# A gated pair of state-space convolutions: decay powers, the negation of v, kept spectra and the gate regrouped, with a new order of work

## The chip, the cores and the metric

The kernel runs on one core of a Trainium2 chip. Such a core has a matrix engine (TensorE, PE in the profile; its weight loads are listed as PEld), a vector engine (VectorE, DVE), an engine for activation functions (ScalarE, ACT), a general one (GpSimd, POOL) and one that issues DMAs here (SyncE, SP). Each runs its own queue in order, and waits on semaphores for the others. The metric is device time of one launch in microseconds (us); less is better.

## The reference

Two state-space convolutions A and B over the same input of 2048 steps by 512 channels, mixed by a gate. Each makes its kernel K from 128 complex modes for a channel, and convolves through an FFT of twice the length:

```python
def ref(u, log_A_real, A_imag, C_real, C_imag, log_dt, D_skip):
    dt = exp(log_dt)
    A = -exp(log_A_real) + 1j * A_imag
    C = (C_real + 1j * C_imag) * dt[:, None]
    P = exp((A * dt[:, None])[:, :, None] * arange(L)[None, None, :])
    K = 2.0 * einsum("dn,dnl->dl", C, P).real
    y = irfft(rfft(u_t, 2 * L) * rfft(K, 2 * L))[..., :L]
    return y_t + u * D_skip

g = sigmoid((x * gate_w).sum(-1, keepdims=True))
return g * ref(x, A_...) + (1 - g) * ref(x, B_...)
```

All data are float32.

## The kernel before

The time axis of 2048 is split in 32 by 64, and the channels of both convolutions (2 x 512) in 64 **units** of 16. Eight units are a **chunk** (parameters of 128 channels of A and B together), two units a pair, and four units a **block**, of which there are 16.

*Parameters.* For chunk 0 alone, and then for the chunks 1 and 2, 3 and 4, 5 and 6, 7, `prep_ops` derives phases and amplitudes; for the later chunks most of it is done on GpSimd (lines 375 to 412). The phases go to DRAM and back in another layout (`bounce`, then `turns`, on the SP queue). `dec` holds two values per mode and channel: the decay rate and the amplitude.

*Bases.* `make_bases` (line 488) makes for each chunk a table `bas` of 28 columns per channel: the powers exp(-s x rate) for s = 0 to 7, 0, 8, ... 56, 0, 64, ... 448 and 0, 512, ... 1536. The zeros are set once; the 24 other columns are one Exp each on ScalarE, of 128 channels, written with a step of 28. `amplitudes` (lines 491, 493, GpSimd) puts in column 24 to 27 the amplitude.

*Units.* For each unit, `phase` (504, TensorE) makes phases in PSUM; ScalarE turns them into sines and cosines (510, 513, 516); `grid0` and `grid1` (520, GpSimd) multiply base columns to decays, 128x1024 and 128x512, into two tiles f0 and f1 of two buffers each; VectorE multiplies decays and sines (543 to 563). `modes` (571, TensorE) sums over the 128 modes, with four column tiles of 32 at a time, into a PSUM tile `pk` of 128x256. `keep` (578, ScalarE) copies it to `ks`, `skip` (581, VectorE) adds the skip weights to its first column. For a pair, `first_k` (593, TensorE) does the first stage of the transform and `keep_x` (600, ScalarE) stores it in `xall`. `inputs` loads and transforms the input of a block in the same way (`load_u` on SP, `first_u`, `keep_u`).

*Blocks.* For a block, `s2` (630, TensorE) does the second stage of the transform in 8 groups; `products` (641, VectorE) multiplies kernel and input spectra; `add_products` (669, on POOL's queue) adds their halves with accumulating DMAs; `inverse` (679, TensorE) transforms back and `keep_z` (685, ScalarE) stores. The spectra of the input, `v`, serve two blocks. They are made ahead for the blocks b + 1 and b + 2 when b is odd, and for blocks 0 and 1 at the start, 8 rounds in all: `keep_v` (650, ScalarE) copies from PSUM, `turn_v` and `both_v` move halves between partitions with DMAs of SP, and `negate_v` (661, VectorE) writes the negative of 64 partitions by 512 columns, four times in a round.

*Ends.* `gate` (760, TensorE, early in the kernel) multiplies the transposed input with the gate's weights: four matmuls for each quarter j, one after another into one PSUM bank, 128 equal output rows; then Sigmoid (765) and a product into the transform's last table (770). `final` (699) and, for the last 128 channels, `last_final` (733) do the last stage; SP writes the result.

*Order.* All this is listed as some 2460 small operations. `ORDER` is a permutation of them, written out in full; they are emitted in that order, and each engine is held to it by extra dependences. `SLOTS` names the PSUM bank, of eight, of each PSUM tile in turn.

Of the kernel before, what the change touches and what calls it, by code (L numbers as in the profile page):

```python
# [29 lines left out]
SHIFTS = list(range(8)) + [8 * b for b in range(8)] + [64 * b for b in range(8)] + [512 * b for b in range(4)]  # L30
# [4 lines left out]
    11, 2, 0, 6, 1, 3, 4, 5, 74, 15, 19, 20, 21, 23, 22, 25, 24, 29, 40, 26, 27, 45, 12, 28, 18,  # L35
    31, 30, 41, 32, 42, 33, 50, 34, 43, 35, 44, 13, 36, 37, 46, 38, 39, 55, 71, 47, 16, 48, 49,
    51, 52, 53, 70, 17, 69, 54, 56, 57, 58, 60, 14, 59, 62, 61, 63, 64, 65, 72, 66, 75, 73, 183,
    67, 83, 68, 78, 84, 82, 7, 79, 8, 85, 192, 9, 10, 147, 323, 80, 77, 210, 81, 76, 191, 86,
    194, 195, 193, 107, 109, 211, 196, 200, 111, 110, 108, 201, 197, 113, 202, 112, 198, 209,
    203, 199, 204, 114, 115, 212, 123, 127, 117, 215, 126, 205, 213, 124, 119, 216, 218, 217,  # L40
    121, 222, 120, 118, 219, 206, 122, 116, 156, 223, 149, 129, 230, 132, 214, 133, 232, 130,
    207, 221, 125, 324, 236, 128, 231, 151, 237, 150, 152, 238, 153, 348, 233, 131, 326, 134,
    157, 89, 234, 87, 158, 208, 235, 239, 90, 155, 325, 93, 243, 88, 161, 160, 220, 162, 148,
    92, 349, 244, 181, 91, 241, 163, 98, 240, 182, 224, 164, 351, 154, 99, 242, 350, 248, 159,
    225, 250, 97, 226, 245, 254, 94, 249, 251, 305, 246, 255, 103, 247, 227, 100, 307, 252, 261,
    102, 306, 229, 258, 135, 256, 96, 257, 228, 253, 262, 95, 165, 308, 260, 311, 166, 259, 104,
    309, 167, 312, 314, 101, 168, 310, 318, 263, 169, 313, 106, 316, 171, 327, 264, 319, 329,
    265, 315, 138, 333, 328, 105, 330, 317, 334, 584, 335, 340, 331, 170, 732, 341, 332, 172,
    136, 336, 175, 173, 337, 320, 338, 174, 352, 321, 354, 339, 139, 322, 137, 342, 358, 353,
    355, 141, 140, 343, 359, 344, 371, 360, 365, 356, 372, 366, 357, 361, 370, 176, 362, 144,  # L50
    177, 363, 373, 364, 178, 376, 374, 377, 379, 179, 383, 378, 741, 180, 380, 184, 375, 384,
    142, 742, 382, 266, 768, 185, 381, 145, 743, 367, 143, 268, 746, 267, 385, 747, 368, 146,
    734, 186, 748, 269, 386, 447, 187, 369, 749, 387, 736, 272, 271, 275, 270, 274, 278, 273,
    276, 281, 277, 280, 284, 283, 188, 282, 287, 286, 290, 285, 289, 279, 452, 189, 291, 453,
    292, 345, 288, 737, 735, 455, 739, 388, 448, 738, 294, 293, 346, 471, 347, 390, 389, 449,
    296, 295, 391, 395, 392, 190, 450, 399, 396, 403, 400, 744, 733, 454, 407, 456, 404, 1317,
    472, 408, 405, 457, 451, 401, 406, 397, 402, 393, 411, 398, 409, 458, 461, 740, 394, 415,
    459, 750, 413, 430, 460, 427, 412, 419, 465, 751, 410, 414, 416, 752, 745, 417, 470, 753,
    421, 418, 466, 767, 297, 473, 756, 420, 462, 476, 424, 474, 463, 299, 477, 423, 464, 478,
# [123 lines left out]
    2396, 2395, 2400, 2399, 2403, 2398, 2402, 2406, 2401, 2405, 2409, 2404, 2407, 2412, 2408,  # L183
    2410, 2415, 2411, 2414, 2312, 2417, 2416, 2413, 2314, 2313, 2421, 2315, 2418, 2419, 2420,
    2422, 2424, 2423, 2426, 2425, 2428, 2427, 2429, 2450, 2453, 2451, 2452, 2456, 2454, 2455,
    2459, 2457, 2458, 2460, 2461,
]


# [807 lines left out]
```

## Time and profile before

| what | value |
|---|---|
| median of 3 runs | 570.46 us |
| lowest and highest run | 565.07, 579.27 us |
| span of the profiled execution, first to last instruction | 568.5 us |
| mean granted TensorE clock | 0.921 of full |
| busy time of PE, DVE, ACT, POOL | 458.2, 412.8, 426.0, 342.6 us |
| HBM read and written | 17.18 and 5.77 MB |

The profile has one execution, of which it gives the span only; the span lies between the lowest and the highest run. Its views are: totals by engine, the chain that ended last (followed back from the last instruction, at each step to what released it), groups of instructions by line with busy time and idle time before them, the timeline, and busy time by stretches. In a group, the busy time is that in which at least one of its instructions ran, so that busy time by count is the pitch of instructions that overlap, while "mean ns" is the full length of one. A float32 matmul is recorded as two instructions.

### The profile page before, as it was taken

To read this page: it belongs to the slowest core of one execution; us is meant where nothing else is said; L and a number is where in the kernel's file an instruction comes from. 1 tells how busy PE (TensorE), PEld (TensorE's weight loads), DVE (VectorE), ACT (ScalarE), POOL (GpSimd) and SP (SyncE) were. 2 spreads that over 40 slices of the span, in tenths; PEclk is the share of its full clock that TensorE was granted. 3 is DMA by queue.
4 is the path that set the end of the run, shared out by engine and by line. 5 is a ranking of instruction groups with operands and counts; after the bars stand their busy time and mean duration, and the time that the engine had idled before them with its cause. 6 is when DMAs were issued, how large, how long until landed. Compare 5 with 4: busy or idle time off the path is not lost.

```text
span 568.5 us, 26964 instructions
## 1 busy us (share of the span) xinstructions
PE 458.2 (81%) x11888; PEld 371.7 (65%) x11888; DVE 412.8 (73%) x826; ACT 426.0 (75%) x967; POOL 342.6 (60%) x324
## 2 busy tenths in 40 slices
PE   8557986879777898868997986968997979859756
PEld 8445456657575676767775774856785757748746
DVE  7096876888967983798689855698689896788210
ACT  4788879969986998867997994949987777565311
POOL 1549986989999877346766653435727664455120
PEclk9797989989988997998999996989997997989779
DMA  3649423460423515044506323044505250163242
GB/s 102 216 130 315 188 58 50 105 131 22 91 48 89 110 38 114 33 98 83 110 7 134 81 51 76 32 96 91 95 21 115 40 96 22 31 131 64 44 74 77
DMA packets 30772, 49.84 MB, mean 88 GB/s; under 512 B 10048, under 2 KB 15680, under 8 KB 30656
## 3 DMA queue, kind: packets, MB, share of 16 engines
q1 hardware_dynamic: 25536, 31.34, 18.6%
q0 software_dynamic: 5120, 16.78, 17.8%
q8 instruction: 93, 1.52, 1.1%
q14 instruction: 23, 0.19, 0.1%
HBM read 17.18 MB, written 5.77 MB: 40 GB/s over the span
## 4 chain that ended last, share of the span: by engine, by line
PE 29%; ACT 17%; DVE 15%; issue 7%; POOL 5%; DMA 1%; ACTq 0%; DVEq 0%; POOLq 0%
PE pk L571 6%; PE psi L679 6%; DVE xall L641 5%; PE p0s L504 5%; DVE v L661 4%; ACT bas L488 4%; PE ps L630 4%; PE ps L593 3%; PE pf L699 3%; ACT xall L600 2%; PE pl L733 1%; ACT p1c L510 1%; ACT z L685 1%; ACT p0c L516 1%; ACT p0c L510 1%
## 5 line engine op out<-in xcount | busy, mean ns | idle before, releaser
L520 POOL TENSOR_TENSOR f<-bas 128x512 f32<-128x512 f32 (+1 forms) x128 | 203.4, 1670 | 119.1 <-PE pk L571 49.3
L630 PE MATMUL ps<-xall,gk 128*64 128x64 f32 (+1 forms) x1728 | 109.4, 252 | 13.3 <-ACT v L650 4.3
L630 PEld LDWEIGHTS ps<-xall,gk 128*64 128x64 f32 (+1 forms) x1728 | 102.4, 155 | 24.8 <-issue 6.6
L641 DVE TENSOR_TENSOR xall<-ps,v 128x256 f32<-128x256 f32 x256 | 91.4, 418 | 26.1 <-PE ps L630 21.1
L571 PE MATMUL pk<-f,f 128*32 128x64 f32 x4096 | 79.1, 231 | 23.7 <-DVE f L551 13.2
L571 PEld LDWEIGHTS pk<-f,f 128*32 128x32 f32 x4096 | 67.3, 117 | 35.0 <-issue 24.4
L669 POOL DMA_DIRECT2D xall<-xall x64 | 60.0, 1203 | 48.0 <-ACT z L685 22.6
L679 PE MATMUL psi<-mi,xall 128*128 128x128 f32 x512 | 74.8, 303 | 11.4 <-DMA xall<-xall 6.8
L679 PEld LDWEIGHTS psi<-mi,xall 128*128 128x128 f32 x512 | 67.8, 211 | 22.5 <-issue 10.7
L559 DVE TENSOR_TENSOR f<-f,p1c 128x512 f32<-128x512 f32 x64 | 43.7, 684 | 25.8 <-ACT p1c L516 23.8
L543 DVE TENSOR_TENSOR f<-f,p0c 128x512 f32<-128x512 f32 x64 | 43.6, 683 | 24.5 <-ACT p0c L516 22.6
L504 PE MATMUL p0s<-cph,ones 64*128 64x512 f16 x128 | 52.8, 412 | 9.2 <-ACT xall L600 3.9
L593 PE MATMUL ps<-w,ks 64*64 64x64 f32 x2048 | 41.9, 231 | 16.2 <-issue 8.1
L685 ACT COPY z<-psi 128x512 f32<-128x512 f32 x64 | 38.5, 620 | 21.5 <-PE psi L679 21.5
L504 PE MATMUL p1s<-cph,ones 64*128 64x512 f16 x128 | 53.0, 414 | 0.7 <-DVE f L559 0.7
L593 PEld LDWEIGHTS ps<-w,ks 64*64 64x64 f32 x2048 | 36.6, 144 | 25.3 <-issue 11.8
L504 PE MATMUL p0s<-cph,rot 64*128 64x512 f16 x128 | 52.4, 409 | 0.2 <-issue 0.2
L504 PE MATMUL p1s<-cph,rot 64*128 64x512 f16 x128 | 52.4, 409 | 0.0
L488 ACT ACTIVATE bas<-dec 128x128 f32<-128x128 f32 x192 | 50.6, 490 | 0.8 <-DVE dec L423 0.7
L510 ACT ACTIVATE p1c<-p1s 128x512 f32<-128x512 f32 x64 | 38.2, 597 | 16.9 <-PE p1s L504 8.1
L510 ACT ACTIVATE p0c<-p0s 128x512 f32<-128x512 f32 x64 | 38.8, 607 | 15.4 <-PE p1s L504 5.7
L563 DVE TENSOR_TENSOR f<-f,p1s 128x512 f32<-128x512 f32 x64 | 43.7, 684 | 5.7 <-ACT p1s L513 4.3
(130 smaller groups left out, 866.7 us busy)
## 6 DMA issues: line engine op xcount, KB each, us to landing
xall<-xall POOLq DMA_DIRECT2D x64, 256.0 KB, 5.3
v<-v SPq DMA_DIRECT2D x64, 128.0 KB, 3.3
uraw<-in_us SPq DMA_DIRECT2D x16, 256.0 KB, 4.2
z<-in_ut SPq DMA_DIRECT2D x16, 256.0 KB, 6.8
out_dram<-ot SPq DMA_DIRECT2D x24, 128.0 KB, 2.4
par<-in_par SPq DMA_DIRECT2D x8, 256.0 KB, 5.2
gk<-in_gk SPq DMA_DIRECT2D x4, 512.0 KB, 7.0
eg<-in_eg SPq DMA_DIRECT2D x4, 512.0 KB, 7.2
```

Of the source, the lines that this page charges most:

```text
L488: S.activation(bas[:, c % 2, :, j], decays[c][:, 0], AF.Exp, scale=-float(s))
L504: PE.matmul(ps, w[h : h + 64], cph[h : h + 64, j], start=j == 0, stop=j == 3, tile_position=(h, 0))
L510: S.activation(pc[u], ps[u], AF.Abs)
L520: G.tensor_tensor(o.rearrange("p k (a b) -> p k a b", b=8), x[:, :, hi : hi + n].unsqueeze(3).to_broadcast([128, 16, n, 8]), x[:, :, lo : ...
L559: V.tensor_tensor(f[:, 0], f[:, 1], p1c[u], OP.mult)
L571: PE.matmul(pk[32 * kd : 32 * kd + 32, i, :], f1[:, p, 4 * i + kd, :], f0[:, p, 4 * i + kd, :], start=p == 1, stop=p == 0, tile_position=( ...
L593: PE.matmul(ps[h][64 * ri : 64 * ri + 64, n, :], x[r], w1[r, ri, r], start=True, stop=True, tile_position=(64 * h, 64 * ri),)
L630: PE.matmul(ps[h : h + w, j, 0:n], gk[:, k, h : h + w], xall[:, x0:x1, 2 * k : 2 * k + 2], start=True, stop=True, tile_position=(0, h),)
L641: V.tensor_tensor(k.rearrange("p x (k t) -> p k x t", t=2), p2s[b, g][:, :, 0:64].rearrange("p k (x t) -> p k x t", t=2), vv.unsqueeze(3). ...
L669: G.dma_start(out=xk(b)[o, s], in_=t2[t, s], accum_op=OP.add)
L679: PE.matmul(ps[:, i, :], xk(b)[:, x : x + 2, :].rearrange("p x k -> p (x k)"), mi, start=True, stop=True)
L685: S.copy(z[:, :, d0 : d0 + 4], pis[b, g].rearrange("p i r -> p r i"))
```

## The change

- *Decay powers.* A new GpSimd product `multiples` makes 1 to 7 times the rate, 128 x 128 x 7, in a tile `rates` of one buffer. `make_bases` is then four Exps for a chunk with scales of -1, -8, -64 and -512: three write 7 columns per channel (896 elements a partition), the fourth 3 (384).
- *Negation.* `negate_v` moves to GpSimd, as a tensor_tensor product with a broadcast column of -1.
- *Kept spectra.* `modes` of the two units of a pair write one PSUM tile of 128x512; `keep` and `skip` run once per pair.
- *Gate.* The four matmuls of a quarter write 32 rows each, in four column tiles; ScalarE copies the result over the input it was made from, and one matmul with a matrix of 1/32 sums the four parts into 128 equal rows.
- *Order.* `inputs` is listed after every second unit of an odd block; `ORDER` (2422 operations now) and `SLOTS` (636 in place of 664) are new throughout.

```diff
-SHIFTS = list(range(8)) + [8 * b for b in range(8)] + [64 * b for b in range(8)] + [512 * b for b in range(4)]
...
+    thirty = const.tile([128, 128], F32, name="thirty")
+    seven = const.tile([128, 7], F32, name="seven")
+    minus = const.tile([128, 1], F32, name="minus")
...
+        V.memset(minus, -1.0)
+        for n in range(7):
+            V.memset(seven[:, n : n + 1], n + 1.0)
+        G.memset(thirty, 1.0 / 32)
...
+    def multiples(c):
+        rates[c] = work.tile([128, 128, 7], F32, name="rates", tag="rates", bufs=1)
+        G.tensor_tensor(
+            rates[c], decays[c][:, 0].unsqueeze(2).to_broadcast([128, 128, 7]),
+            seven.unsqueeze(1).to_broadcast([128, 128, 7]), OP.mult,
+        )
+
     def make_bases(c, n):
-        for j, s in list(enumerate(SHIFTS))[10 * n : 10 * n + 10]:
-            if s:
-                S.activation(bas[:, c % 2, :, j], decays[c][:, 0], AF.Exp, scale=-float(s))
+        j, w = 8 * n + 1, 7 if n < 3 else 3
+        S.activation(bas[:, c % 2, :, j : j + w], rates[c][:, :, 0:w], AF.Exp, scale=-float(8**n))
...
     def modes(u):
         f0, f1 = f0s[u], f1s[u]
-        pks[u] = pk = bank("pk")[:, 0:256].rearrange("p (i j) -> p i j", i=4)
+        q, h = divmod(u, 2)
+        if h == 0:
+            pks[q] = bank("pk", (128, 8, 64))
...
-                        pk[32 * kd : 32 * kd + 32, i, :], f1[:, p, 4 * i + kd, :], f0[:, p, 4 * i + kd, :],
-                        start=p == 1, stop=p == 0, tile_position=(0, 32 * kd),
+                        pks[q][32 * kd : 32 * kd + 32, 4 * h + i, :], f1[:, p, 4 * i + kd, :],
+                        f0[:, p, 4 * i + kd, :], start=p == 1, stop=p == 0, tile_position=(0, 32 * kd),
...
-    def keep(u):
-        kss[u] = work.tile([128, 4, Q], F32, name="ks", tag="ks", bufs=4)
-        S.copy(kss[u], pks[u])
-
-    def skip(u):
-        V.tensor_tensor(kss[u][:, :, 0], pks[u][:, :, 0], dl[:, 4 * u : 4 * u + 4], OP.add)
+    def keep(q):
+        kss[q] = work.tile([128, 8, Q], F32, name="ks", tag="ks", bufs=2)
+        S.copy(kss[q], pks[q])
+
+    def skip(q):
+        V.tensor_tensor(kss[q][:, :, 0], pks[q][:, :, 0], dl[:, 8 * q : 8 * q + 8], OP.add)
...
     def negate_v(i, h):
-        V.tensor_scalar(v_at(hi, i, 1, h), v_at(hi, i, 0, h), -1.0, None, op0=OP.mult)
+        x = v_at(hi, i, 0, h)
+        G.tensor_tensor(v_at(hi, i, 1, h), x, minus[hi].unsqueeze(2).to_broadcast(x.shape), OP.mult)
...
-    def gate(j):
+    def gate_parts(j):
         psg[j] = bank("psg")
         for sb in range(nsb):
             PE.matmul(
-                psg[j], gw[:, sb : sb + 1].to_broadcast([128, 128]), ut(sb, j), start=sb == 0, stop=sb == nsb - 1
+                psg[j][32 * sb : 32 * sb + 32], gw[:, sb : sb + 1].to_broadcast([128, 32]), ut(sb, j),
+                start=True, stop=True, tile_position=(0, 32 * sb),
             )
+
+    def gate_keep(j):
+        S.copy(ut(0, j), psg[j])
+
+    def gate(j):
+        psg[j] = bank("psg")
+        PE.matmul(psg[j], thirty, ut(0, j), start=True, stop=True)
...
     def chunk(c):
         op("ro", turns, c)
-        for n in range(3):
+        op("mu", multiples, c)
+        for n in range(4):
             op("ex", make_bases, c, n)
...
         if u % 2:
-            op("f1", first_k, u // 2)
+            q = u // 2
+            op("ke", keep, q)
+            op("kd", skip, q)
+            op("f1", first_k, q)
...
-        if b % 2 and n < 2 and b < nblk - 1:
-            inputs(b + 1 + n)
+        if b % 2 and n % 2 and b < nblk - 1:
+            inputs(b + 1 + n // 2)
```

28 lines of the change are left out of this document (10 added, 18 removed), and 293 rows, old and new, of tables (ORDER, SLOTS).

## The prediction

> **What bounds the kernel now.** I read the totals first, then the chain that ended last, then the groups of instructions and the order of time around the pieces the chain names. Totals and the chain by engine:
>
> ```profile
> span 568.5 us, 26964 instructions
> PE 458.2 (81%) x11888; PEld 371.7 (65%) x11888; DVE 412.8 (73%) x826; ACT 426.0 (75%) x967; POOL 342.6 (60%) x324
> PE 29%; ACT 17%; DVE 15%; issue 7%; POOL 5%; DMA 1%; ACTq 0%; DVEq 0%; POOLq 0%
> ```
>
> No engine is full. TensorE is busy 81% of the span, and the chain passes from engine to engine, so the time is set by waits between queues that are each run in a fixed order. The chain of waits by line:
>
> ```profile
> by line: issue 7.2%; PE pk L571 6.2%; PE psi L679 5.8%; DVE xall L641 4.6%; PE p0s L504 4.6%; DVE v L661 4.3%; ACT bas L488 4.1%; PE ps L630 3.8%; PE ps L593 3.4%; PE pf L699 3.3%; ACT xall L600 1.6%; PE pl L733 1.4%; ACT p1c L510 1.3%; ACT
> ```
>
> Two entries stand out, because they are no heavy arithmetic: the negation of v (DVE L661, 4.3% of 568.5 = 24.4 us) and the Exps of the decay powers (ACT L488, 4.1% = 23.3 us). The groups of instructions show how large they are as a whole, and give the durations used below (the columns are busy time, mean ns of one, then the idle time ahead of it):
>
> ```profile
> L520 POOL TENSOR_TENSOR f<-bas 128x1024 f32<-128x1024 f32 x64 | 136.2, 2129 | 10.4 <-ACT bas L488 6.5 <-PE pk L571 3.9
> L571 PE MATMUL pk<-f,f 128*32 128x64 f32 x4096 | 79.1, 231 | 23.7 <-DVE f L551 13.2 <-issue 8.2 <-DVE f L555 1.1
> L520 POOL TENSOR_TENSOR f<-bas 128x512 f32<-128x512 f32 x64 | 76.9, 1211 | 108.7 <-PE pk L571 45.3 <-issue 23.4 <-DVE f L543 16.9
> L488 ACT ACTIVATE bas<-dec 128x128 f32<-128x128 f32 x192 | 50.6, 490 | 0.8 <-DVE dec L423 0.7
> L661 DVE TENSOR_SCALAR v<-v 64x512 f32<-64x512 f32 x32 | 41.1, 1298 | 0.8
> L600 ACT COPY xall<-ps 128x512 f32<-128x512 f32 x64 | 36.2, 616 | 10.5 <-PE ps L593 10.3
> L578 ACT COPY ks<-pk 128x256 f32<-128x256 f32 x64 | 25.6, 402 | 28.2 <-PE pk L571 28.1
> L760 PE MATMUL psg<-z,small 128*128 128x512 f32 x32 | 14.8, 605 | 0.0
> L581 DVE TENSOR_TENSOR ks<-pk,dl 128x4 f32<-128x4 f32 x64 | 10.3, 161 | 35.3 <-ACT ks L578 34.9
> L383 POOL TENSOR_TENSOR tb<-tb,sg 128x256 f32<-128x256 f32 x12 | 10.0, 831 | 0.5
> L488 ACT ACT_TABLE_LOAD x6 | 7.7, 1283 | 0.1
> ```
>
> The negation's mean is 1298 ns, with 64 partitions by 512 columns. One that runs undisturbed takes a third of that. The order of time around unit 28 shows why:
>
> ```profile
> 247.52 0.42 DVE L661 TENSOR_SCALAR v<-v 64x512 f32<-64x512 f32 x1
> ...
> 250.66 4.79 DVE L661 TENSOR_SCALAR v<-v 64x512 f32<-64x512 f32 x2
> 250.66 1.36 POOL L520 TENSOR_TENSOR f<-bas 128x512 f32<-128x512 f32 x1
> 251.67 1.16 POOL L669 DMA_DIRECT2D xall<-xall  x1
> 252.26 2.55 POOL L520 TENSOR_TENSOR f<-bas 128x1024 f32<-128x1024 f32 x1
> ...
> 255.48 0.69 DVE L547 TENSOR_TENSOR f<-f,p0c 128x512 f32<-128x512 f32 x1
> 256.22 1.59 PE L593 MATMUL psu<-w,uraw 64*64 64x64 f32 x64 [4.46 <-DVE f L547]
> ```
>
> With POOL idle the negation takes 0.42 us (247.52). At 250.66 two of them start with a POOL grid and are over only after POOL's next 128x1024 grid has ended (252.26 + 2.55 = 254.81). The DVE does nothing else for 4.79 us, and TensorE then stands 4.46 us, released by the DVE instruction behind the negations. The same picture, three more times:
>
> ```profile
> 306.82 2.56 DVE L661 TENSOR_SCALAR v<-v 64x512 f32<-64x512 f32 x1
> 310.25 1.10 PE L571 MATMUL pk<-f,f 128*32 128x64 f32 x64 [3.51 <-DVE f L551]
> ...
> 376.33 4.78 DVE L661 TENSOR_SCALAR v<-v 64x512 f32<-64x512 f32 x2
> 381.89 1.99 PE L593 MATMUL psu<-w,uraw 64*64 64x64 f32 x64 [4.45 <-DVE f L547]
> ...
> 497.45 3.62 DVE L661 TENSOR_SCALAR v<-v 64x512 f32<-64x512 f32 x1
> 503.01 1.24 PE L593 MATMUL ps<-w,ks 64*64 64x64 f32 x36 [4.77 <-DVE f L555]
> ```
>
> **The change part by part.** The sums are made against the profiled execution's span of 568.5 us. The page gives no other time of that execution; the median of the three runs, 570.46 us, is 2.0 us above the span, and I add these 2 us at the end.
>
> *1, negation to POOL.* DVE loses all 32 L661 instructions, 41.1 us. The four stalls above cost TensorE 4.46 + 3.51 + 4.45 + 4.77 = 17.2 us of standing. TensorE stands 19% of the span anyway (100 less 81), so of these 17.2 us I count 81%, **14 us gained**. The ends: nothing, if TensorE is held by the next late thing; 24.4 us, the negation's whole share of the chain. I take 14 since it is read off TensorE itself. On POOL a negation is a tensor_tensor of 512 columns with a broadcast operand; the nearest row is the 128x512 grid, also with broadcast operands, 76.9 / 64 = 1.20 us (the plain 128x256 product's 831 ns is the lower bound, two of these the upper one). 32 x 1.20 = 38 us more on POOL.
>
> *2, Exps.* Before, a chunk needs 24 Exps of 128 columns: 50.6 / 192 = 0.263 us each when back to back, 6.3 us a chunk. After: three of 896 columns and one of 384. Between 0.263 us for 128 columns and 36.2 / 64 = 0.566 us for 512 (L600) lie 0.79 ns a column, so 0.87 us and 0.47 us, 3.1 us a chunk; by L600's mean of 616 ns for 512 columns alone, 1.08 and 0.46, 3.7 us. I take 3.4: 2.9 us saved in each of 8 chunks, 23 us of ACT. Of the 50.6 us, 23.3 are on the chain, 46%, so at most 10.7 us can come off the end; nothing, if ACT's next work waits for TensorE anyway. I take half, 5.4. The new order changes between Exp, Sin and Sigmoid 22 times where the old one did 21 times by my count of both lists (chunk 5's four Exps are cut in two by unit 32's sines), so one load of 1.28 us more. **4 us gained.** In front of the Exps stands a new POOL product of 896 columns: between the grid rows, 1.20 us at 512 and 136.2 / 64 = 2.13 us at 1024, that is 1.9 us, 15 us for 8. Its tile has one buffer, so the product for chunk 2 waits on POOL until chunk 1's four Exps are done. Behind it in POOL's queue stand the added products of block 0 and then unit 8's grids; the grids read these very Exps, so the wait adds nothing to them.
>
> The load's own row, and the Exps behind it:
>
> ```profile
> 329.52 1.28 ACT L488 ACT_TABLE_LOAD   x1
> 330.82 6.42 ACT L488 ACTIVATE bas<-dec 128x128 f32<-128x128 f32 x24
> ```
>
> The Exps start 0.02 us after the load has ended. The Trainium skill ("ScalarE: Activation LUTs", What ACT_TABLE_LOAD costs) sets 2.66 us for a switch, a load and a drain of 1.38 us. By that the extra switch would cost 1.4 us more than I count; these two rows show no such gap.
>
> *3, two units per kept spectrum.* 64 copies of 256 columns (25.6 us) become 32 of 512 at 0.566, 18 us: 7 us off ACT; 64 additions (10.3 us) become 32: 5 us off DVE. Neither line is among the chain's entries of over 1%. On the other side a PSUM bank is now held over two units, and the first unit's kernel spectrum waits for the second unit. Between 3 us either way I take **1 us gained**.
>
> *4, gate.* 16 products of 512 columns, 14.8 us of TensorE. On four column tiles, the four of a gate can run side by side: the modes (L571) do so, 64 columns in 79.1 / 4096 = 19 ns where 14.8 / 32 = 462 ns for 512 columns make 58 ns for 64. Then 3.7 us, 3.7 us for the four summing products, and four ACT copies, 2.3 us, ahead of which TensorE has other work in the new list. 7.4 us less, at most; TensorE idles 19% of the span and more work waits behind ACT and DVE there, so **1 us gained**, and 4 us lost if the tiles ran one behind the other.
>
> *5, POOL as a whole.* 38 + 15 = 53 us more. Its busy time in two stretches (the columns are PE, PEld, DVE, ACT, POOL):
>
> ```profile
> 40.00:200.00 160.00, 126.52 (x2906) 95.57 (x2908) 126.08 (x240) 137.12 (x311) 141.89 (x144) 0.94 0.43 110
> 200.00:480.00 280.00, 238.20 (x6786) 192.93 (x6787) 218.36 (x424) 223.05 (x512) 156.92 (x140) 0.92 0.35 72
> ```
>
> From 200 on POOL has 280 - 157 = 123 us to spare: the cover is there. From 40 to 200 it has 18 us. Up to unit 21, where that stretch ends, the new list puts 9 negations and 3 products there, 9 x 1.20 + 3 x 1.9 = 16.5 us. But it also moves the preparation of chunks 5 and 6 out: 25 POOL instructions stand ahead of unit 18's grids in the old list, 4 ahead of the grids of unit 21 in the new one; at 0.83 us these 21 are 17 us. So this stretch stays as full as it was. What is not covered is a grid that is due at once and now has a negation in front of it; a tenth of 53 us, **5 us lost**, between 0 and the 53 themselves.
>
> *6, the rest of the order.* All lists are new, also those of SP and of POOL's accumulating DMAs; the number of DMAs stays (156 issues of SP, 64 of POOL). Two places can be priced. Preparation for chunk 7 goes late: its bounce to DRAM and back now stands on SP behind three transfers of v of block 11, which wait for ACT's copies; it is due at unit 56, four units on, so it is covered. And the end:
>
> ```profile
> 526.12 1.50 PE L593 MATMUL ps<-w,ks 64*64 64x64 f32 x85
> 531.13 1.54 PE L593 MATMUL ps<-w,ks 64*64 64x64 f32 x43 [3.51 <-issue]
> 532.60 3.78 PE L679 MATMUL psi<-mi,xall 128*128 128x128 f32 x16
> 536.31 5.20 PE L630 MATMUL ps<-xall,gk 128*64 128x64 f32 x128
> 541.44 2.17 PE L679 MATMUL psi<-mi,xall 128*128 128x128 f32 x16
> 543.35 3.32 POOL L669 DMA_DIRECT2D xall<-xall  x4 [15.22 <-ACT z L685]
> 550.42 5.42 PE L679 MATMUL psi<-mi,xall 128*128 128x128 f32 x32 [6.82 <-DMA xall<-xall]
> ```
>
> Here all is serial: last spectra (L593), block 14's first two inverses (532.60), block 15's second stage (536.31), its products, POOL's accumulating DMA, block 15's inverses (550.42). The new list puts all four inverses of block 14 behind the second stage, where 6.82 us of waiting for the DMA cover them: 536.31 - 532.60, **3.7 us gained**. What else the order does I can't price; I put it at 10 us either way in the range.
>
> Sum: 568.5 - 14 - 4 - 1 - 1 + 5 - 3.7 = 549.8, and 2 for the median: 552 us.
>
> **The rivals.** *Hidden:* DVE and ACT are relieved, but TensorE's own work sets the pace. It falls from 458.2 to 450.8 us; at today's span per busy us, 568.5 / 458.2 = 1.24, the span is 559, the time 561. For it: PE has the largest share of the chain, 29%. Against: the four stalls stand on TensorE itself.
>
> *All of it:* the whole chain shares come off, 24.4 + 10.7 + 3.7 = 38.8, time 532. Against: with 7 to 8 us a unit on three engines, another wait is seldom far behind.
>
> *POOL blocks:* a negation must wait for ACT's copies of v, and in POOL's fixed order everything behind it waits too, the grids of the next units above all. POOL has paid for such a wait already, ahead of an accumulating DMA:
>
> ```profile
> 375.74 0.86 POOL L669 DMA_DIRECT2D xall<-xall  x1 [6.85 <-ACT v L650]
> ```
>
> If each of the 8 rounds of negations holds POOL so long, 8 x 6.85 = 55 us, the gains (23.7 without the 5 us lost) are eaten and the time is 570.5 - 23.7 + 55 = 602; it is over 2% slower from 35 us, 4.4 us a round. Against: the new list places a round's four negations apart, up to 12 units late, after the copies are due. The Trainium skill ("GPSIMD Engine Reference", Engine selection) speaks against this move as well: elementwise work belongs on VectorE, with GpSimd about twice as slow for two inputs. By that factor a negation would be 0.84 us and POOL's load 11 us smaller than mine. The rows agree with the direction, 1.20 against 0.42 us, yet the 0.42 us held only while POOL was idle.
>
> **How the numbers follow.** About 2% (11 us) is what a measurement of this kernel can tell from no change: faster is below 559, slower above 582. My forecast of 538 to 559 has 0.50, all of it (below 538) 0.14, hidden (559 to 582) 0.24, POOL blocks (over 582) 0.12. Faster is 0.50 + 0.14. The range 533 to 574 leaves out most of the blocked case, and the ends of two others.
>
> **What would show it.** In the profile after: no POOL-long DVE instruction of v; negations on POOL at 1.1 to 1.3 us; DVE busy about 367 us, ACT near 397, POOL near 395, PE near 451; Exps in groups of some 3.4 us a chunk; second stage of block 15 directly behind the last L593. I am wrong if POOL's waits for ACT's copies of v, or for TensorE's modes, grow by more than 25 us, or if TensorE's idle time stays at 110 us.

## The result, and the profile after

The changed kernel takes 509.47 us (median of 4 runs, 502.11 to 512.51), against 570.44 us of the kernel before in the same comparison (565.07 to 579.27). The ratio is 0.887, with a 95% interval from 0.877 to 0.896: 11% faster. Ratios, here and below, are made from the faster executions of each kernel alone, medians from all: for the changed kernel the faster two, 502.11 and 507.36 us, make the gain 65 us, and the profile below is of an execution of 511.58 us. By the medians it is 61 us, where 18 us were forecast; the time lies below the range (533 to 574), and 23 us below the rival that took the whole chain shares off. The direction was right, the size was not.

Totals of the changed kernel, and its chain that ended last, by engine:

```profile
span 509.8 us, 26782 instructions
PE 441.0 (87%) x11896; PEld 356.5 (70%) x11896; DVE 369.9 (73%) x770; ACT 402.7 (79%) x780; POOL 386.8 (76%) x365
PE 50%; DMA 10%; issue 10%; DVE 10%; POOL 9%; ACT 9%; SPq 0%; DVEq 0%; POOLq 0%; ACTq 0%
```

The busy times came out nearly as forecast: VectorE 369.9 us (forecast 367), ScalarE 402.7 (397), GpSimd 386.8 (395), TensorE 441.0 (451). So the work that each part moves was counted well. What was not forecast is how closely TensorE is kept fed: it is busy 87% of the span, not 81%, and half of the chain is now its own, not 29%. The groups of the parts that changed (busy time, mean ns of one, idle time before):

```profile
L653 POOL TENSOR_TENSOR v<-v,minus 64x512 f32<-64x512 f32 x32 | 33.1, 1042 | 8.4 <-issue 6.4
L470 POOL TENSOR_TENSOR rates<-dec,seven 128x896 f32<-128x896 f32 x8 | 14.5, 1812 | 0.0
L477 ACT ACTIVATE bas<-rates 128x896 f32<-128x896 f32 x24 | 22.2, 969 | 0.1
L477 ACT ACTIVATE bas<-rates 128x384 f32<-128x384 f32 x8 | 5.0, 620 | 0.0
L569 ACT COPY ks<-pk 128x512 f32<-128x512 f32 x32 | 19.8, 618 | 14.2 <-PE pk L562 14.2
L572 DVE TENSOR_TENSOR ks<-pk,dl 128x8 f32<-128x8 f32 x32 | 5.3, 167 | 7.0 <-ACT ks L569 6.8
L752 PE MATMUL psg<-z,small 128*32 128x512 f32 x32 | 5.1, 704 | 0.0
L762 PE MATMUL psg<-z,thirty 128*128 128x512 f32 x8 | 6.3, 882 | 0.0
L562 PE MATMUL pk<-f,f 128*32 128x64 f32 x4096 | 76.3, 226 | 14.0 <-issue 9.1 <-ACT p1s L502 2.1 <-DVE f L552 1.2
L509 POOL TENSOR_TENSOR f<-bas 128x1024 f32<-128x1024 f32 x64 | 134.5, 2112 | 28.7 <-PE pk L562 17.7 <-issue 10.4
L509 POOL TENSOR_TENSOR f<-bas 128x512 f32<-128x512 f32 x64 | 78.1, 1226 | 19.8 <-issue 8.5 <-PE pk L562 7.2 <-DVE xall L632 3.1
```

A negation on GpSimd takes 1.03 us by its pitch (33.1 / 32; forecast 1.20), a product of rates 1.81 (forecast 1.9), the Exps 27.2 us for 8 chunks (22.2 + 5.0), which is 3.4 a chunk as forecast. The gate takes 5.1 + 6.3 = 11.4 us of TensorE, 3.4 less than before and not 7.4 less. That is in part the clock: one of the four quarters and two of the four sums ran at a granted clock of 0.50 to 0.56 and took 1.85 to 2.07 us each, the others 1.06 to 1.13 us at 1.00. In a run below with the same gate (e3) the two lines take 4.3 and 4.5 us. The last two rows show how GpSimd makes room: it stands 19.8 + 28.7 = 48.5 us ahead of its grids, where it stood 108.7 + 10.4 = 119.1 us before, although it has 44 us more to do. By the same two rows it stands 94.2 us with the old work in the new order (e1) and 79.8 us with the negation alone moved in the old one (e7), so the order and the negation both have a part in this.

Where TensorE stands behind VectorE's multiplications, the longest groups before (above) and after (below), from the view of waits: total us, times, longest:

```profile
PE pk L571 <- DVE f L551: 13.2, 6, 3.6
PE psu L593 <- DVE f L547: 8.9, 2, 4.5
PE psu L593 <- DVE f L559: 6.7, 2, 6.3
PE ps L593 <- DVE f L555: 4.8, 1, 4.8
```

```profile
PE ps L621 <- DVE f L540: 1.3, 2, 0.7
PE pk L562 <- DVE f L552: 1.2, 3, 0.4
PE p1s L493 <- DVE f L548: 0.8, 1, 0.8
```

Added up over all rows of that view, by the engine and the tile named as releaser, TensorE's idle time in the kernels that the text below compares is (us; "mult." are VectorE's multiplications into f, "issue" is time in which the profile shows no wait; waits too short for a row are left out, so that busy and idle time come to a few us less than the span):

```
kernel (profiled run)                  span  PE busy  PE idle | mult. issue  ACT   DMA  DVE ks  clock
before                                568.5   458.2    104.4  |  44.6  24.1  19.2  12.2   0.9   0.921
old order, three parts (e2)           567.2   451.2    111.0  |  26.6  31.6  24.0  20.3   5.3   0.925
old order, negation on GpSimd (e7)    559.4   452.6    101.6  |  26.3  27.7  18.9  21.4   3.4   0.930
old order, four Exps (e9)             571.4   457.0    108.9  |  44.4  28.5  19.2  12.8   0.6   0.922
old order, products regrouped (e12)   578.1   462.8    109.5  |  32.4  28.3  20.6  19.0   3.9   0.914
old order, preparation spread (e13)   609.5   471.2    132.7  |  49.2  25.8  26.1  12.3  16.1   0.888
new order, old work (e1)              535.1   456.6     72.7  |  19.9  18.9   9.7  10.2   6.7   0.946
after                                 509.8   441.0     63.9  |   8.6  29.1  10.1   9.1   5.2   0.959
```

Of the 58.7 us between the two spans, 40.5 are idle time of TensorE and 17.2 are its busy time. Of the 17.2, the gate accounts for 3.4; in the rest the same matmuls run shorter (the 4096 records of the modes 76.3 us, 79.1 before), at a granted clock of 0.959 in place of 0.921. The clock was higher in nearly every kernel in which TensorE stood less; whether it follows from that was not tried. By the ratio of the clocks alone 458.2 us would become 440.0, near the 441.0 measured; but for the new order with the old work (e1) it gives 446.1, and 456.6 was measured. So the clock fits here, and is not the whole account.

The stretches of the prediction, after the change (columns as there: PE, PEld, DVE, ACT, POOL, then clock, DMA share, GB/s):

```profile
40.00:200.00 160.00, 137.23 (x3557) 102.33 (x3561) 130.71 (x249) 142.21 (x268) 148.87 (x141) 0.95 0.39 88
200.00:480.00 280.00, 251.01 (x7214) 206.89 (x7205) 206.45 (x419) 219.58 (x434) 207.40 (x188) 0.96 0.39 83
```

TensorE is busy 137 of 160 us from 40 to 200, where it was 127, and 251 of 280 us behind, where it was 238. The gain is not in one place: the last kept spectrum of unit 9 comes at 103.7 us (120.7 before), of unit 31 at 254.7 (285.0), of unit 63 at 476.1 (526.6), and the end at 509.8 (568.5). These are 17, 13, 20 and 8 us by stretch.

### The profile page after: what moved, and what is told of

It is laid out like the page before. It is cut to its first block, busy times and chain, and to the rows that moved or that the text cites. A ratio compares the mean times of both kernels' runs of the same rounds, so it can differ in the third digit from the quotient of the medians.

```text
span 509.8 us, 26782 instructions
## 1 busy us (share of the span) xinstructions
PE 441.0 (87%) x11896; PEld 356.5 (70%) x11896; DVE 369.9 (73%) x770; ACT 402.7 (79%) x780; POOL 386.8 (76%) x365
## 4 chain that ended last, share of the span: by engine, by line
PE 50%; DMA 10%; issue 10%; DVE 10%; POOL 9%; ACT 9%; SPq 0%; DVEq 0%; POOLq 0%; ACTq 0%
PE ps L621 14%; PE pk L562 9%; PE psi L671 8%; DMA xall<-xall 7%; PE p0s L493 6%; POOL f L509 4%; DVE xall L632 4%; PE ps L584 3%; POOL xall L661 3%; PE pf L691 3%; PE psu L584 2%; PE pl L725 2%; DMA uraw<-in_us 1%; ACT xall L591 1%; DVE f L552 1%
## 5 line engine op out<-in xcount | busy, mean ns | idle before, releaser
L509 POOL TENSOR_TENSOR f<-bas 128x1024 f32<-128x1024 f32 (+1 forms) x128 | 204.0, 1669 | 48.5 <-PE pk L562 25.0
L621 PE MATMUL ps<-xall,gk 128*64 128x64 f32 (+1 forms) x1728 | 114.0, 254 | 9.3 <-issue 3.1
L562 PE MATMUL pk<-f,f 128*32 128x64 f32 x4096 | 76.3, 226 | 14.0 <-issue 9.1
L562 PEld LDWEIGHTS pk<-f,f 128*32 128x32 f32 x4096 | 64.7, 113 | 28.0 <-issue 18.6
L671 PE MATMUL psi<-mi,xall 128*128 128x128 f32 x512 | 70.9, 288 | 8.7 <-DMA xall<-xall 2.9
L671 PEld LDWEIGHTS psi<-mi,xall 128*128 128x128 f32 x512 | 62.5, 196 | 18.3 <-issue 4.7
L536 DVE TENSOR_TENSOR f<-f,p0c 128x512 f32<-128x512 f32 x64 | 43.7, 683 | 26.1 <-ACT p0c L505 23.6
L532 DVE TENSOR_TENSOR f<-f,p0c 128x512 f32<-128x512 f32 x64 | 43.6, 681 | 10.5 <-POOL f L509 5.2
L584 PE MATMUL ps<-w,ks 64*64 64x64 f32 x2048 | 38.9, 223 | 12.1 <-issue 6.6
L584 PEld LDWEIGHTS ps<-w,ks 64*64 64x64 f32 x2048 | 34.3, 136 | 19.7 <-issue 9.2
L544 DVE SCALAR_TENSOR_TENSOR f<-f,p0s 128x512 f32<-128x512 f32 x64 | 43.6, 681 | 5.0 <-ACT p0s L502 3.9
## 6 DMA issues: line engine op xcount, KB each, us to landing
xall<-xall POOLq DMA_DIRECT2D x64, 256.0 KB, 5.8
z<-in_ut SPq DMA_DIRECT2D x16, 256.0 KB, 5.5
uraw<-in_us SPq DMA_DIRECT2D x16, 256.0 KB, 3.7
par<-in_par SPq DMA_DIRECT2D x8, 256.0 KB, 5.5
```

The costliest lines, as they stand in the source:

```text
L509: G.tensor_tensor(o.rearrange("p k (a b) -> p k a b", b=8), x[:, :, hi : hi + n].unsqueeze(3).to_broadcast([128, 16, n, 8]), x[:, :, lo : ...
L532: V.tensor_tensor(f0[:, 0, :, 0:32], f0[:, 1, :, 0:32], half(u, p0c[u], True), OP.mult)
L536: V.tensor_tensor(f0[:, 0, :, 32:64], f0[:, 1, :, 32:64], half(u, p0c[u], False), OP.mult)
L562: PE.matmul(pks[q][32 * kd : 32 * kd + 32, 4 * h + i, :], f1[:, p, 4 * i + kd, :], f0[:, p, 4 * i + kd, :], start=p == 1, stop=p == 0, til ...
L584: PE.matmul(ps[h][64 * ri : 64 * ri + 64, n, :], x[r], w1[r, ri, r], start=True, stop=True, tile_position=(64 * h, 64 * ri),)
L621: PE.matmul(ps[h : h + w, j, 0:n], gk[:, k, h : h + w], xall[:, x0:x1, 2 * k : 2 * k + 2], start=True, stop=True, tile_position=(0, h),)
```

## The experiments

*All old work in the new order (e1), and three of the four parts in the old order (e2).* Nearly the two halves of the change. e1 is the changed kernel with the parts' work put back; the pair's kernel spectra still share one PSUM tile, since the new list is written for that:

```diff
-            rates[c], decays[c][:, 0].unsqueeze(2).to_broadcast([128, 128, 7]),
...
-        S.activation(bas[:, c % 2, :, j : j + w], rates[c][:, :, 0:w], AF.Exp, scale=-float(8**n))
+        for k in range(w):
+            S.activation(bas[:, c % 2, :, j + k], decays[c][:, 0], AF.Exp, scale=-float((k + 1) * 8**n))
...
-        S.copy(kss[q], pks[q])
+        for h in range(2):
+            S.copy(kss[q][:, 4 * h : 4 * h + 4], pks[q][:, 4 * h : 4 * h + 4])
...
-        G.tensor_tensor(v_at(hi, i, 1, h), x, minus[hi].unsqueeze(2).to_broadcast(x.shape), OP.mult)
+        V.tensor_scalar(v_at(hi, i, 1, h), v_at(hi, i, 0, h), -1.0, None, op0=OP.mult)
...
+                psg[j], gw[:, sb : sb + 1].to_broadcast([128, 128]), ut(sb, j), start=sb == 0, stop=sb == nsb - 1
```

e2 is the kernel before, with its list of operations, and the changed Exps with their product, negation and gate; kernel spectra are still kept unit by unit, so that the third part is missing.

> The new order with the old work: 24 Exps of 128 columns for a chunk, the negation on VectorE as a tensor_scalar, two copies and two additions for a pair, the old gate. Theory A (the order carries what the forecast missed, some 40 us; the four parts give some 18): about 528 us, 0.925 of before. Theory B (the parts carry nearly all, the order little): 560 us or more, 0.98 or more. Theory C (the order fits only the new work, both are needed): not below 550 us here and not below 540 us with the parts alone.

> The old order with the new work of three parts: four Exps and a POOL product for a chunk, the negation on POOL, the gate on four column tiles, each at the place where the old order had the old work (kept spectra stay one unit at a time, since a bank held over two units can't be fitted to the old list of banks). Theory A: 545 to 555 us, 0.96 of before. Theory B: 510 to 525 us. Theory C: 540 to 565 us.

Measured: e1 535.39 us, ratio 0.939 (0.935 to 0.943); e2 570.07 us, ratio 1.000 (0.996 to 1.003). So 35 us come with the order (with its banks and its shared PSUM tile), nothing with three parts alone, and 61 with everything: the parts are worth 26 us by the medians, 30 by the ratios, but only in the new order. Of the theories the first came nearest for e1 (528), and none has e2's 570. In e2 the stalls behind the negation are gone as forecast (idle time behind VectorE's multiplications 44.6 to 26.6 us), and the time comes back under other names: issue +7.5, ScalarE +4.8, DMA +8.1, kept spectra +4.4.

*One part back in the changed kernel (e3, e4, e5, e6).* e3 puts the negation back on VectorE, e4 the 24 Exps of a chunk, e5 the two copies and additions of a pair, each with the lines of the diff above. e6 puts the gate's old matmuls back:

```diff
-        psg[j] = bank("psg")
-        for sb in range(nsb):
-            PE.matmul(
-                psg[j][32 * sb : 32 * sb + 32], gw[:, sb : sb + 1].to_broadcast([128, 32]), ut(sb, j),
-                start=True, stop=True, tile_position=(0, 32 * sb),
-            )
...
-        S.copy(ut(0, j), psg[j])
...
-        PE.matmul(psg[j], thirty, ut(0, j), start=True, stop=True)
+        for sb in range(nsb):
+            PE.matmul(
+                psg[j], gw[:, sb : sb + 1].to_broadcast([128, 128]), ut(sb, j), start=sb == 0, stop=sb == nsb - 1
+            )
```

> The changed kernel with only the negation back on VectorE. If the stalls behind POOL's running instruction are worth what the forecast gave them, 14 us more than the changed kernel, about 523 us, with L661-like instructions of 1 to 4 us on DVE. If another wait takes their place, under 4 us more. If POOL's relief by 33 us counts for more than the stalls, faster than the changed kernel.

> The changed kernel with only the 24 Exps of 128 columns for a chunk back and POOL's product gone. Forecast's theory: 4 to 6 us more than the changed kernel, about 515 us. Rival, that ACT is close to the bound in the first 200 us, where five of the eight chunks' Exps lie: 15 us or more, 525 us.

> The changed kernel; only the copy and the skip addition of a pair's kernel spectrum are made in two halves, one for each unit (64 copies of 256 columns and 64 additions again, at the same places in the list; the PSUM tile is still one for a pair). The prediction's step: 1 us slower (510.5). If the kept spectra carry the remainder of the 26 us that the parts are worth in the new order: 515 to 520. By busy time, 7 us more on ScalarE and 5 us on VectorE, of which as large a share as of the Exps' 23 us (11 us came off the end) would be 3 to 6 us: 513 to 515.

> The changed kernel with the gate's old matmuls: four for each quarter into one bank, and neither the copy nor the summing matmul. The prediction's step: 1 us slower (510.5); without ScalarE's copy in front of the sigmoid it may also be up to 2 us faster. If the gate carries the remainder of the parts' 26 us: 515 or more.

Measured: e3 514.67 us (ratio 0.900, 0.895 to 0.906), e4 520.61 (0.906, 0.899 to 0.912), e5 510.51 (0.890, 0.883 to 0.897), e6 510.38 (0.884, 0.876 to 0.893). Against the changed kernel (509.47 us, 0.887) the negation is worth 5 us by the medians and 8 by the ratios, the Exps 11 by either, the copies 1 or 2 and the gate 1 or -1, which can't be told from nothing. The Exps' loss is clear of the scatter; the negation's interval just touches that of the changed kernel (0.877 to 0.896). Each of the two lies between the values that its theories give. One by one that makes 18 of the 26 us by the medians, 19 of 30 by the ratios; whether the rest comes only when several are undone together, or is scatter, is not shown. Why the negation is worth so little here, one row for each kernel suggests (durations: least, median, longest ns):

```profile
L661 DVE TENSOR_SCALAR v<-v x32: 418/698/4454, 32.5 to 501.8; 64x512 f32<-64x512 f32 x32
```

```profile
L652 DVE TENSOR_SCALAR v<-v x32: 418/576/2493, 34.1 to 467.8; 64x512 f32<-64x512 f32 x32
```

```profile
L653 POOL TENSOR_TENSOR v<-v,minus x32: 1032/1038/1072, 32.7 to 462.0; 64x512 f32<-64x512 f32 x32
```

Before, a negation on VectorE took up to 4.45 us. With the same instruction in the new list (e3) the longest takes 2.49 us and the median falls from 698 to 576 ns; already with all the old work in the new order (e1) the 32 take 24.4 us, 41.1 before. That fits a new order that meets fewer of GpSimd's long instructions; the meetings were not counted. On GpSimd a negation takes 1.03 to 1.07 us here. The Trainium skill ("SBUF — State Buffer", SBUF: two separate sides) says that VectorE in some modes and GpSimd exclude each other from a shared port for a whole instruction, and do not share its rate. The 4.45 us agree with that, and are longer than one 128x1024 grid of GpSimd (2.13 us by the mean) and the 0.42 us together, so that such a negation was held up over more than one instruction. The Trainium skill's rule against the move ("GPSIMD Engine Reference", Engine selection), elementwise work on VectorE, held for one instruction, 1.04 us against 0.42, and not for the kernel, which is 5 to 8 us slower with the quicker instruction.

*The negation alone, and the Exps alone, in the old order (e7, e9).*

```diff
-        V.tensor_scalar(v_at(hi, i, 1, h), v_at(hi, i, 0, h), -1.0, None, op0=OP.mult)
+        x = v_at(hi, i, 0, h)
+        G.tensor_tensor(v_at(hi, i, 1, h), x, minus[hi].unsqueeze(2).to_broadcast(x.shape), OP.mult)
```

That is e7. e9 instead makes the product of rates ahead of a chunk's first Exps, and four Exps at the three old places, the first two at the first.

> The kernel before with one edit: the negation of v on GpSimd as a product with a broadcast column of -1; old order, old Exps, old gate. By the prediction's first step this alone gains 14 us (556). Theory I (in the old order the relief of VectorE is taken up by grids that come late behind the negations): between 562 and 570, with TensorE's idle time behind VectorE's multiplications down by 14 to 18 us and VectorE's wait for grids up by over 10 us.

> The kernel before with only the four Exps and POOL's product for a chunk. Forecast: 4 to 6 us less, 565 us. Theory P: no gain or a loss of some us, since the Exps now wait for a product in POOL's full queue.

Measured: e7 564.53 us, ratio 0.990 (0.985 to 0.994), 6 us faster where the prediction's step has 14; e9 576.12, ratio 1.009 (1.004 to 1.014), slower. e7's waits, with the same two of the kernel before below:

```profile
DVE f L550 <- POOL f L527: 22.4, 14, 3.4
PE psi L687 <- DMA xall<-xall: 10.7, 4, 6.8
PE psu L600 <- DMA uraw<-in_us: 8.0, 2, 4.7
```

```profile
PE psi L679 <- DMA xall<-xall: 6.8, 1, 6.8
PE psu L593 <- DMA uraw<-in_us: 2.9, 1, 2.9
```

VectorE, no longer held up, now waits 22.4 us for GpSimd's grids (32.3 us over all its multiplications, 3.1 before), and TensorE 9 us longer for transfers (10.7 + 8.0 against 6.8 + 2.9). The stall was real, and 18.3 us of idle time behind it went; the waits that took its place read as those of a list whose work is placed for the old pace. In e9 the Exps wait 9.5 us for the new product, which GpSimd does late:

```profile
ACT bas L501 <- POOL rates L495: 9.5, 5, 3.4
```

*The end of the list (e11).* The prediction's own step for the end, in the kernel before: block 14's first two inverses and their copies go behind block 15's second stage.

```diff
 ... first_k(31), keep_x(31, 0), keep_x(31, 1)
-inverse(14, 0), keep_z(14, 0), inverse(14, 1), keep_z(14, 1)
 s2(15, 0) to s2(15, 7)
+inverse(14, 0), keep_z(14, 0), inverse(14, 1), keep_z(14, 1)
 inverse(14, 2), ...
```

> The kernel before with only block 14's first two inverses (and their copies) moved behind block 15's second stage. Forecast: 3.7 us less, 566 to 567 us. The new order's end is 8 us shorter than the old one's; if this move is all of it, 562 us.

Measured: 570.25 us, ratio 1.001 (0.998 to 1.004): no gain. TensorE's last pieces in e11, and in the changed kernel (start, us, group, idle time before it):

```profile
526.77 1.50 PE L589 MATMUL ps<-w,ks 64*64 64x64 f32 x85
531.64 1.54 PE L589 MATMUL ps<-w,ks 64*64 64x64 f32 x43 [3.38 <-issue]
534.34 5.89 PE L626 MATMUL ps<-xall,gk 128*64 128x64 f32 x128 [1.16 <-ACT xall L596]
549.13 6.37 PE L675 MATMUL psi<-mi,xall 128*128 128x128 f32 x32 [4.18 <-DMA xall<-xall]
```

```profile
475.41 2.14 PE L584 MATMUL ps<-w,ks 64*64 64x64 f32 x128
480.36 3.97 PE L621 MATMUL ps<-xall,gk 128*64 128x64 f32 x107 [0.57 <-issue]
489.34 2.05 PE L671 MATMUL psi<-mi,xall 128*128 128x128 f32 x16 [0.87 <-ACT z L677]
492.64 2.02 PE L671 MATMUL psi<-mi,xall 128*128 128x128 f32 x16 [1.25 <-ACT z L677]
495.48 2.02 PE L671 MATMUL psi<-mi,xall 128*128 128x128 f32 x16 [0.81 <-DMA xall<-xall]
```

In e11 the wait for the last transfer is shorter as forecast, 4.18 us for 6.82, and the second stage starts 2 us earlier, but it takes 5.89 us for 5.20, and the last 32 inverse records take 6.37 for 5.42. From the last modes to the end the kernel before has 43.4 us and the changed one 35.4; that gain of 8 us comes from other things: the last first stage takes 2.14 us there and no gap of 3.38 us stands in it, and behind block 14's last inverses (489.34) block 15's come in two halves that wait 1.25 and 0.81 us, the second for the transfer that cost 6.82 us before.

*One queue of the old list, changed alone (e10, e10b, e12, e13, e14, e17).* These look for what in the new list carries its 35 us. In e10b the preparation of chunks 5 to 7 on all its engines is moved later, towards its places in the new list; e10 is the same in e2. In e12, on VectorE alone, the products that interrupt a unit's six multiplications go behind them:

```diff
 one_cos(30), one_sin(30), cos_minus(30), skip(29)
-three products of block 6
 cos_plus(30)
-two products of block 6
 sin_plus(30)
-eleven products of block 6
 sin_minus(30)
+the sixteen products of block 6
```

In e13, on GpSimd alone, preparation is spread among the grids; e14 has both; in e17 only the PSUM banks are dealt out anew.

> The parts in the old order (as in the run with the parts alone), but with the preparation of chunks 5, 6 and 7 moved to later units, as the new order has it; all else in the old order. Theory P (in the old order the parts gain nothing since POOL, loaded with this preparation from 40 to 260 us, takes their load on top): 545 to 555 us, unit 27 some 15 us earlier than with the parts alone. Theory Q (the old order's other waits keep the time, whatever POOL does): 565 us or more.

> The kernel before with only that preparation moved later, old work otherwise. If the preparation's place already cost time before: 560 us or less. If POOL had just enough room: 566 to 572 us, no change.

> The kernel before; on VectorE alone the spectra products and negations that stand between the first and the last of a unit's six multiplications are moved behind the last one where the other queues' old order allows it: 205 such interruptions become 86 (the new list has 125). All work and all other queues are as before (some PSUM banks change). Theory V (the new order gains because VectorE finishes a unit's multiplications in one go): 535 to 558 us, and TensorE's idle time released by VectorE's multiplications falls from 44.6 us to under 30. Theory Q (no single queue carries the gain): within 4 us of 570, and that idle time falls by under 8 us or is replaced by idle time of the same size on another releaser.

> The kernel before; on GpSimd alone the preparation of the later chunks is spread: where over two of its instructions stand ahead of a grid, the surplus goes behind that grid (runs of up to 15 ahead of a grid become runs of 2, with three longer ones left). All work and all other queues are as before. Theory G (the new order gains because a grid no longer waits behind a run of preparation on GpSimd): 545 to 562 us, and TensorE's idle time released by VectorE's multiplications, which read those grids, falls by over 10 us from 44.6 us. Theory Q (no single queue carries the gain): within 4 us of 570.

> The two edits together: VectorE's products behind the units' multiplications, and GpSimd's preparation spread, in the kernel before. If V and G each carry a part, the gains add up and the time comes near the 535 us of the new order with the old work. Theory Q: still within 6 us of 570, since the matrix queue and ScalarE's copies keep their old places and pass on the wait.

> The kernel before with its old list of operations; only the PSUM banks are dealt out anew (of the free banks always the one that has been free longest; 572 of 664 tiles change bank). Theory B (the new list gains by its banks: TensorE waits less for banks to come free): at least 10 us faster, under 560. Otherwise: within 5 us of 570.

Measured:

```
e10   595.04 us   ratio 1.045 (1.042 to 1.048)
e10b  592.58 us   ratio 1.040 (1.036 to 1.045)
e12   579.59 us   ratio 1.018 (1.012 to 1.024)
e13   610.73 us   ratio 1.068 (1.063 to 1.074)
e14   616.89 us   against 570.26 of the kernel before
e17   565.27 us   ratio 0.988 (0.980 to 0.996)
```

No edit to one queue gains, so the theories that name VectorE's or GpSimd's queue fall. Those of no change fall too: e10b, e12, e13 and e14 are 9 to 47 us slower than the kernel before. In e12 the idle time behind VectorE's multiplications does fall, 44.6 to 32.4 us (its theory asks for under 30), and the time still gets worse: DMA, issue and kept spectra take 14 us more (table above). In e13 GpSimd's surplus is late for ScalarE, and its grids then wait for TensorE:

```profile
POOL f L516 <- PE pk L567: 82.2, 22, 7.5
ACT sp L392 <- POOL tb L379: 24.2, 3, 15.5
```

The first of these waits was 49.3 us before. This reads as an old list whose queues are fitted to each other: where GpSimd's or VectorE's is moved alone, other engines wait for it. TensorE's and ScalarE's queues were not moved alone. Other banks alone give 6 us (571.45 less 565.27; 3 to 11 by the interval), a sixth of the order's gain; they are not the new list's banks.

*Half of each list (e15, e16).* The kernel before's work, one list up to the phases of unit 32 and the other behind them. The kernel spectra are kept unit by unit here, each unit in a PSUM tile of its own, also in the half that follows the new list.

```diff
-ORDER = old list
+ORDER = old list up to phase(32), then the rest by the new list     (e15)
+ORDER = new list up to phase(32), then the rest by the old list     (e16)
```

> The kernel before's work; the old list up to the phases of unit 32, behind them all other operations in the new list's order and banks (kernel spectra kept per unit throughout). Theory L (the new order gains in each stretch by itself): the new order with the old work gained 14.4 us up to unit 31's kept spectrum and 35 us in all, so about 20 us stay: 550. Theory H (a lead gained early in the new list carries the rest): within 5 us of 570.

> The mirror: the new list's order up to the phases of unit 32, the old one behind them, the kernel before's work. Theory L: the first half's 14.4 us stay: 556. Theory H: 535 to 545, as the early lead carries on. Theory J (the queues of either list fit only as a whole): slower than 565, the first half's gain being lost at the joint.

Measured: e15 577.02 us, ratio 1.011 (1.007 to 1.016); e16 593.35, ratio 1.028 (1.017 to 1.040). Neither keeps any gain, which looks like the third theory, that a list fits only as a whole. But e16 has lost its lead ahead of the joint: kept spectra of unit 13 at 139.9 us (136.0 in e1, which runs the same list), of unit 23 at 215.5 (203.1), of unit 27 at 256.0 (237.6; 250.1 before). The loss at unit 27 is 8%, where the executions of e16 differ by 2% (585.34 to 597.31 us). TensorE's longest waits in that stretch, e16 and then e1:

```profile
PE pk L567 <- issue: 4.3, 2, 2.4
PE pk L567 <- DVE f L555: 3.8, 2, 2.7
PE ps L626 <- ACT v L646: 3.7, 1, 3.7
PE ps L589 <- DVE ks L577: 3.4, 2, 2.8
PE pk L567 <- ACT v L646: 2.8, 1, 2.8
PE ps L626 <- DVE xall L637: 2.2, 3, 0.9
...
PE pk L567 <- DVE xall L637: 1.7, 2, 1.3
```

```profile
PE ps L584 <- DVE ks L572: 4.7, 2, 4.2
PE p0s L490 <- ACT xall L591: 1.5, 1, 1.5
```

Waits on ScalarE's copies to v and VectorE's products make 10.4 us here, of a loss of 18 us on the way to unit 27; e1 has 0.4 us of them. The second stage and the modes do not read what these write; so they can only wait there for the PSUM bank that these release. Two tiles for a pair, both held to the end of the pair, leave the new list a bank less than it was made for, and some other tiles had to change bank with them. So these two runs don't separate the theories; what e16 suggests is that the new list rests on the pair's shared tile, which the prediction had counted as a cost.

*A version with fewer table loads (e18).* In the changed kernel, chunk 5's second Exp goes to the other three ahead of unit 32's sines, and chunk 1's last Exp ahead of the fourth Sigmoid:

```diff
 make_bases(5, 2)
+make_bases(5, 1)
 ...
 sine of unit 33, 34
-make_bases(5, 1)
```

> The changed kernel; chunk 5's second Exp joins the three others ahead of unit 32's sines, and chunk 1's last Exp goes ahead of the fourth Sigmoid: three table loads of 1.28 us fewer. If each load stands on the path: 509.5 less 3.8, that is 505.7. If other work hides them: within 2 us of 509.5. Slower by over 2 us would mean that the Exps now hold up the sines of unit 32.

Measured: 508.74 us, ratio 0.888 (0.880 to 0.896), the same as the changed kernel. The list has 22 table loads in place of 23, not 20: chunk 1's Exp, moved alone, brought a switch of its own. A load of 1.28 us fewer can't be seen here.

## Why the prediction was wrong

The step that failed is the sixth, *the rest of the order*: "What else the order does I can't price; I put it at 10 us either way in the range." Alone, with the old work, the order measured 35 us, three and a half times that bound; and the four parts, 15 us net in the sum (14 + 4 + 1 + 1 - 5), were added to it as if they held in any order, when three of them make nothing in the old one (e2) and the four make 26 to 30 us in the new one. Both errors have, as we read them, one root. The prediction priced instructions, and took the 104 us in which TensorE stands as a given, of which edits could remove single stalls. But they belonged in part to the list: with the same work in the new list (e1) 72.7 us are left. 10 us was no bound from the trace, which showed 104.

By its steps:

- *Negation.* The mechanism was right: the long negations are gone, and in the old order the idle time behind VectorE's multiplications fell by 18.3 us (e7), where the four stalls quoted made 17.2. But the size was off: 14 us forecast, 6 measured in the old order, 5 to 8 in the new. The step took 81% of the stall as gained, since TensorE is busy 81% of the time; but what was late next, transfers (9.2 us more of TensorE's idle time in e7), issue (3.6) and kept spectra (2.5), took back 15 of the 18 us. The rest of the gain in that trace is TensorE's busy time, 5.6 us less (452.6 for 458.2).
- *Exps.* The duration was right (3.4 us a chunk). The worth was not: 4 us forecast, 11 in the new order, and in the old one a loss of 5 to 6. The one table load more came as counted (23 against 22). That the product of rates adds no wait held only for the new list; in the old one the Exps waited 9.5 us for it (e9).
- *Kept spectra and gate.* 1 us each forecast; undone, 1 us each by the medians, too little to tell from nothing. The kept spectra's other side was seen with the wrong sign: the shared PSUM tile was counted as a bank held longer, and e16 suggests that it is a bank saved, on which the new list rests.
- *GpSimd as a whole.* Its load came out nearly as counted (386.8 us, 395 forecast), and the cover held: GpSimd stands 48.5 us ahead of its grids, and stood 119.1. No run shows the 5 us charged for it in the new order. In the old one e7 shows such a loss, VectorE's waits for grids.
- *The end.* 3.7 us forecast for one move, which alone gives nothing (e11); the end as a whole gained 8.

Of the rivals, *hidden* is refuted by the 61 us, and *POOL blocks* by its own sign: POOL's waits for ScalarE's copies of v fell from 13.7 to 4.8 us, those for the modes from 49.3 to 25.0; *all of it* had the right side but stopped at the chain shares, 38.8 us. TensorE's idle time did not stay at 110 us, which the prediction named as its test; by the same count, span less busy time, it fell to 69, much further than the named stalls.

What stays open is which trait of the new list carries the 35 us. A new deal of the banks in the old list gives 6 us of it, the tried edits to VectorE's and GpSimd's queues and the move at the end give none; the queues of TensorE and ScalarE were not tried alone. The half lists could not say whether it is gained stretch by stretch, because of the tile; a half list with the pair's shared tile was not run.

## What to carry to other kernels

Where queues run in a fixed order and no engine is full, the idle time of the busiest engine is about the most that a new order can bring, as long as that engine's busy time stays (in e1 31.7 of the 33.4 us between the spans were idle time); put that in the range, and not a round figure. An edit's worth belongs to the order it is made in: three of the parts made 0 us in one list and all four 26 in another, so a part that measures nothing alone should be measured again after the order is made anew, and a part that relieves an engine can bring little until the work behind it is moved up. In a fitted list a queue rearranged alone can cost time even where it shortens the wait that it aims at, as in e12.

## What was not expected of the hardware

- The same negation takes 0.42 to 4.45 us on VectorE, the long ones beside GpSimd's grids in the stretches read, and on GpSimd 1.03 to 1.07 us in the changed kernel, up to 1.33 in e2 and e7.
- TensorE's granted clock differs between orders of the same work: 0.921 before, 0.946 with the new order and the old work, 0.888 with GpSimd's preparation spread (over the executions 0.909 to 0.938, 0.946 to 0.965 and 0.875 to 0.889).
- A gap that no wait explains stands in the last first stage, of 3.4 to 3.5 us after 85 records in the kernel before, e7, e9 and e11, and of 1.1 to 4.1 us in all other runs that keep the kernel spectra unit by unit. Where the pair shares its PSUM tile, in the changed kernel and in e1, e3 to e6 and e18, no gap there is longer than 0.4 us. Its cause was not found.
- The granted clock moves within a kernel, too: the same eight records of a quarter of the gate took 1.06 us at a clock of 1.00 and 1.85 us at 0.55.
